# Window attention and a softplus feed-forward: new due times in the planner, weight words loaded ahead, and one VectorE step less per weight block

## The chip, the cores and the metric

The kernel runs on one NeuronCore of a Trainium2 chip, as one program. The metric is the device time of one execution in microseconds; the median of several runs is given. Times of single instructions come from one profiled execution.

The engines are called by their names: TensorE (PE, matrix products; PEld are its weight loads), VectorE (DVE), ScalarE (ACT), GpSimd (POOL) and SyncE (SP), which in this kernel issues nearly all DMA transfers.

## What is computed

```python
# q, k, v: 8 x 8 heads x 576 positions x 64; w_in 512 x 2048, w_out 2048 x 512
scores = q @ k.T / 8, masked to 0 <= pos_q - pos_k < 64
attn   = softmax(scores)            # with + 1e-9 in the denominator
x      = (attn @ v), heads side by side     # 4608 tokens x 512
h      = x @ w_in
g      = max(h, 0) + log1p(exp(-abs(h)))    # softplus
out    = g @ w_out                          # 4608 x 512, float32
```

The weights arrive as 64-bit floats and are handed to the kernel as pairs of 32-bit words (`w_words`): the upper word holds the sign, 11 bits of exponent and 20 bits of fraction, the lower word the rest. The kernel turns them into 32-bit floats itself.

## The kernel before

**Tiling.** The 4608 tokens are cut into 12 groups of 384. For each group, attention is made for four pairs of heads (`attention(g, hp)`), and the feed-forward runs over 16 blocks of 128 inner units (`ffn`). A block has an up-projection U (12 matmuls of 384 columns, L574), softplus on ScalarE (absolute value, exponential, logarithm, L578 to L580) and VectorE (the max and the sum, L586), a split of the result into a high and a low part (L588, L589), and a down-projection D (9 matmuls of 512 columns, L598) that adds up in PSUM over the 16 blocks. All products of the feed-forward are made as three products of high and low parts.

**The first two groups** go in a special order: blocks 0 to 7 of group 0, all 16 of group 1, then blocks 8 to 15 of group 0, so that the second half of the weights is needed later. The partial sums of group 0 wait in DRAM meanwhile (L636 and following). The attention of groups 0 and 1 turns the scores on TensorE (L439) and multiplies in 32 bits (L450). From group 2 on the scores are split into three bf16 parts and turned by DMA transposes (L475), and the products run at L542.

**Weights.** `convert(f)` handles block f. SP loads the words of a block (1 MB, L247) into a buffer that belongs to this block alone. ScalarE takes the absolute value of the upper word, read as a float (L248). Five VectorE steps follow: a maximum with 2^-15 (L249), a shift by three with a mask (L250), the two upper bits put in (L252), the three bits from the lower word put in (L254), and, after ScalarE has rounded the result to the high part (L256), the difference as the low part (L257). The work buffers are two, and the output's staging shares them.

**The order of work.** Nothing is left to a compiler. Every step above is an `Op` with an engine, a planned cost, the steps it depends on and the buffers that it opens or uses. `arrange` plays the kernel through with these costs: of all steps that could start on the engine that is free first, it takes the one with the earliest due time. The list that comes out is the order in which each engine's instructions are issued; the planned times themselves are not kept on the chip, where an engine goes through its list and waits only for data and buffers. A step on SP is not planned earlier than 30 us before it is due (`EARLY`). A transfer's length comes from a modelled pipe (`BYTES_PER_US`).

Due times come from `dues(times)`: U of step n is due at a time from the last round's plan, D 6.3 us later, the x of a group `AHEAD` (1, 1, 8 and 8 us) before its first U, and each pair of heads `APART` (4, 6, 18, 19 us) before the next. From there they are carried back along the dependencies, each step's cost stretched by 1.4. After each of four rounds the starting times of the U become the new `times`, and the plan that ends first is kept.

Of the kernel before, what the change touches and what calls it, by code (L numbers as in the profile page):

```python
# [8 lines left out]
F32 = mybir.dt.float32  # L9
# [6 lines left out]
P = 128  # L16
# [10 lines left out]
ROUNDS = 4  # L27
# [4 lines left out]
EARLY = 30  # L32

ZERO_HIGH = 2.0**-15

RESULT = {"PE": 0.25, "DVE": 0.12, "ACT": 0.15, "POOL": 0.2, "SP": 2.0}
BYTES_PER_US = 260e3
SMALL = 400e3
# [17 lines left out]
class Op:  # L56
    def __init__(self, eng, cost, fn, deps=(), opens=(), uses=(), nbytes=0, name=""):
        self.eng, self.cost, self.fn, self.name, self.nbytes = eng, cost, fn, name, nbytes
        self.deps, self.opens = [d for d in deps if d is not None], list(opens)
        self.due = self.start = self.end = 0.0  # L60
        self.later = []
        for d in self.deps:
            d.later.append(self)
        for b in [*uses, *opens]:
            b.users.append(self)


def arrange(ops, rings):
# [3 lines left out]
    free = {"PE": 0.0, "DVE": 0.8, "ACT": 2.1, "POOL": 0.8, "SP": 0.8}  # L72
    pipe = 0.0
# [4 lines left out]
    order = []  # L78
    while len(order) < len(ops):
        best = None  # L80
        for e, waiting in open_ops.items():
            could = []
            for o in waiting:
                at = max(ready_at[id(o)], o.due - EARLY if e == "SP" else 0.0)
                taken = {}
                for b in o.opens:
                    r = b.ring
                    n = len(r.taken) + taken.get(id(r), 0) - r.n
                    taken[id(r)] = taken.get(id(r), 0) + 1
                    if n >= 0:  # L90
                        users = r.taken[n].users
# [12 lines left out]
        if best is None:  # L104
            raise ValueError("stuck: " + ", ".join(o.name for w in open_ops.values() for o in w)[:600])
        t, o = best
        o.start = t
        free[o.eng] = t + o.cost
        o.end = t + o.cost + RESULT[o.eng]
        if o.nbytes:  # L110
            pipe = max(pipe, t + o.cost) + o.nbytes / BYTES_PER_US
            o.end = max(t + o.cost + 1.6 * o.nbytes / BYTES_PER_US, pipe if o.nbytes > SMALL else 0.0) + RESULT["SP"]
        for b in o.opens:
            b.ring.taken.append(b)
        done.add(id(o))
        order.append(o)
        open_ops[o.eng].remove(o)
        for n in o.later:
            left[id(n)] -= 1
            ready_at[id(n)] = max(ready_at[id(n)], t + o.cost if n.eng == o.eng and not o.nbytes else o.end)  # L120
            if not left[id(n)]:
                open_ops[n.eng].append(n)
    return order


@with_exitstack
def window_attention_softplus_ffn(
# [109 lines left out]
    def convert(f):  # L237
# [10 lines left out]
        a = add("ACT", 1.05, lambda: nc.scalar.activation(work(), word(1).bitcast(F32), AF.Abs), deps=[a], opens=[work], uses=[raw], name=f"abs{f}")  # L248
        a = add("DVE", 0.6, lambda: ts(work(), work(), ZERO_HIGH, None, ALU.max), deps=[a], uses=[work], name=f"c1.{f}")  # L249
        a = add("DVE", 0.6, lambda: ts(bits(), bits(), 3, 0x3FFFFFF8, ALU.logical_shift_left, ALU.bitwise_and),  # L250
                deps=[a], uses=[work], name=f"c2.{f}")
        a = add("DVE", 1.13, lambda: stt(bits(), word(1), 0xC0000000, bits(), ALU.bitwise_and, ALU.bitwise_or),  # L252
# [13 lines left out]
    def attention(g, hp):  # L266
# [27 lines left out]
        if quad:  # L294
# [29 lines left out]
            s = add("PE", 1.65, scores, deps=[lq, lk], opens=[*sp, st, mn], uses=[slot, two["q_in"], two["k_in"], *far], name=f"S{tag}")  # L324
# [87 lines left out]
        if by_pe:  # L412
# [42 lines left out]
            pv = add("PE", 1.65, products, deps=cp + lv, opens=[av, *x_t], uses=[pt, v_now, *both], name=f"V{tag}")  # L455
# [47 lines left out]
        c4 = add("DVE", 1.0, lambda: tt(v3()[low, :, :, 0, :], vv()[low, :, :, :], v12()[low, :, :, 1, :], ALU.subtract),  # L503
                 deps=[c3], opens=[v3], uses=[v_in, v12], name=f"v3.{tag}")
        c5 = add("DVE", 0.41, lambda: nc.vector.tensor_copy(v3()[up, :, :, 0, :], v12()[up, :, :, 0, :]), deps=[c1, c4],
# [4 lines left out]
        for hh in range(2):  # L510
# [38 lines left out]
            y = add("ACT", 0.39, lambda ds=ds, av=av: nc.scalar.copy(xf()[ds, :], av()[D:P, :TB]), deps=[p],  # L549
                    uses=[av, xf], name=f"y0.{tag}")  # L550
            done.append(add("DVE", 0.47, lambda ds=ds, av=av: tt(xf()[ds, :], av()[0:D, :TB], xf()[ds, :], ALU.add),  # L551
# [12 lines left out]
    def ffn(n, g, f, first, last):  # L564
# [20 lines left out]
        s = add("ACT", 1.21, soft, deps=[a], opens=[u], uses=[hps], name=f"soft{g}.{f}")  # L585
# [99 lines left out]
    best = None  # L685
    for _ in range(ROUNDS):
        for (p, n), r in rings.items():
            r.held = [b for key, b in two.items() if b.ring is r]
        dues(times)
# [4 lines left out]
        times = [o.start for o in ups]  # L694
# [48 lines left out]
```

## Time and profile before

| what | value |
|---|---|
| median of 3 runs | 994.69 us (994.53 to 995.12) |
| the profiled execution's own time | 993.75 us |
| its span, first to last instruction | 991.9 us |
| TensorE busy | 950.3 us, 96% of the span |
| VectorE busy | 796.2 us, 80% |
| ScalarE busy | 744.8 us, 75% |
| mean granted clock of TensorE | 0.987 |

A row of instructions gives the line of the kernel, engine, operation, written and read buffers, sizes and count. In groups, the total busy time and the mean of one in ns follow, then the idle time of the engine just before them and what ended it. In a timeline, the first number is the start, the second the length, both in us from the start of the span; a bracket at the end is the idle time before the row and its releaser. In a table of stretches each engine has its busy time and count, then come the granted clock of TensorE, the mean busy share of 16 DMA engines and GB/s. In a list of waits, the columns are total us, times, and the longest.

### The profile page before, as it was taken

To read this page: it belongs to the slowest core of one execution; us is meant where nothing else is said; L and a number is where in the kernel's file an instruction comes from. 1 tells how busy PE (TensorE), PEld (TensorE's weight loads), DVE (VectorE), ACT (ScalarE), POOL (GpSimd) and SP (SyncE) were. 2 spreads that over 40 slices of the span, in tenths; PEclk is the share of its full clock that TensorE was granted. 3 is DMA by queue.
4 is the path that set the end of the run, shared out by engine and by line. 5 is a ranking of instruction groups with operands and counts; after the bars stand their busy time and mean duration, and the time that the engine had idled before them with its cause. 6 is when DMAs were issued, how large, how long until landed. Compare 5 with 4: busy or idle time off the path is not lost.

```text
span 991.9 us, 16876 instructions
## 1 busy us (share of the span) xinstructions
PE 950.3 (96%) x6128; PEld 847.9 (85%) x6128; DVE 796.2 (80%) x1776; ACT 744.8 (75%) x1685; POOL 4.5 (0%) x18
## 2 busy tenths in 40 slices
PE   4888998999999999999999999999999999999997
PEld 3777977988898899989988988889888888988996
DVE  8995999788888888888888888878988888875333
ACT  6787887777778878877788788877877887776443
POOL 1000000000000000000000000000000000000000
PEclk7899998999999999999999999999999999999999
DMA  9606624554454345546444535444444645631000
GB/s 353 241 1 237 220 54 102 151 169 108 113 133 120 86 112 139 122 101 134 104 120 126 127 88 142 109 120 128 110 103 118 137 101 102 148 55 32 33 1 33
DMA packets 196516, 117.37 MB, mean 118 GB/s; under 512 B 130192, under 2 KB 187536, under 8 KB 194384
## 3 DMA queue, kind: packets, MB, share of 16 engines
q1 hardware_dynamic: 196144, 115.90, 45.4%
q8 instruction: 48, 0.79, 0.3%
q10 hardware_dynamic: 288, 0.39, 0.1%
q14 instruction: 36, 0.29, 0.1%
HBM read 74.58 MB, written 10.22 MB: 85 GB/s over the span
## 4 chain that ended last, share of the span: by engine, by line
PE 69%; ACT 16%; DVE 11%; issue 3%; DMA 1%; POOL 0%; SPq 0%; ACTq 0%; POOLq 0%; DVEq 0%
PE ps_o L598 31%; PE ps_h L574 30%; ACT st L388 4%; PE ps_a L542 3%; PE ps_a L363 3%; ACT u L579 2%; ACT u L578 2%; DVE u L586 1%; ACT xf L549 1%; DVE st L290 1%; ACT v L500 1%; DVE work L252 1%; DVE w L257 1%; ACT k L351 1%; ACT u L580 1%
## 5 line engine op out<-in xcount | busy, mean ns | idle before, releaser
L574 PE MATMUL ps_h<-x,w 128*128 128x384 f32 x2304 | 436.5, 339 | 11.8 <-DVE u L586 10.9
L598 PE MATMUL ps_o<-w,g 128*128 128x512 f32 x1728 | 433.9, 397 | 5.2 <-DVE g L589 3.4
L574 PEld LDWEIGHTS ps_h<-x,w 128*128 128x128 f32 x2304 | 404.1, 189 | 25.6 <-DVE u L586 7.9
L598 PEld LDWEIGHTS ps_o<-w,g 128*128 128x128 f32 x1728 | 315.0, 188 | 73.8 <-DVE g L589 14.6
L578 ACT ACTIVATE u<-ps_h 128x384 f32<-128x384 f32 x192 | 93.3, 486 | 127.4 <-PE ps_h L574 126.1
L586 DVE SCALAR_TENSOR_TENSOR u<-ps_h,u 128x384 f32<-128x384 f32 x192 | 106.6, 555 | 83.3 <-ACT u L580 81.5
L388 ACT ACTIVATE st<-st,mn 128x128 f32<-128x128 f32 x288 | 111.8, 390 | 19.2 <-DVE st L380 11.7
L589 DVE TENSOR_TENSOR g<-u,g 128x384 fp32r<-128x384 f32 x192 | 106.6, 555 | 13.0 <-ACT g L588 8.4
L580 ACT ACTIVATE u<-u 128x384 f32<-128x384 f32 x192 | 100.9, 526 | 6.1
L579 ACT ACTIVATE u<-u 128x384 f32<-128x384 f32 x192 | 100.8, 525 | 6.1
L588 ACT CAST g<-u 128x384 fp32r<-128x384 f32 x112 | 56.6, 505 | 15.8 <-DVE u L586 15.7
L290 DVE CUSTOM_DVE_ANT_0 st<-ps_a,wide 128x192 f32<-128x192 f32 x176 | 53.6, 351 | 14.2 <-PE ps_a L363 13.3
L542 PEld LDWEIGHTS <-v 128*128 128x128 bf16 x1136 | 54.7, 98 | 9.7 <-issue 9.1
L542 PE MATMUL ps_a<-tr,v 128*128 128x128 bf16 (+1 forms) x1136 | 61.5, 211 | 0.0
L363 PEld LDWEIGHTS ps_a<-k,q_hl 128*128 128x128 f32 x432 | 57.8, 191 | 2.9
L363 PE MATMUL ps_a<-k,q_hl 128*128 128x192 f32 x432 | 57.5, 271 | 0.0
L503 DVE TENSOR_TENSOR v<-v_in,v 64x896 bf16<-64x896 f32 x40 | 43.6, 1090 | 13.4 <-ACT v L502 12.8
L388 ACT ACTIVATION_READ_ACCUMULATOR st<-st,mn 128x1 f32 x288 | 53.9, 187 | 0.0
L351 ACT CAST k<-k_in 128x896 fp32r<-128x896 f32 x36 | 33.6, 934 | 24.6 <-PE ps_a L363 24.2
L502 ACT CAST v<-v_in 128x896 bf16<-128x896 f32 x40 | 37.4, 934 | 16.8 <-DVE v_in L501 16.8
L551 DVE TENSOR_TENSOR xf<-ps_a,xf 64x384 f32<-64x384 f32 x80 | 44.0, 550 | 4.7 <-ACT xf L549 2.5
L403 DVE TENSOR_TENSOR st<-st,sm 128x768 f32<-128x768 f32 x48 | 45.8, 954 | 0.9
(78 smaller groups left out, 778.1 us busy)
## 6 DMA issues: line engine op xcount, KB each, us to landing
v_in<-in_v_dram SPq DMA_DIRECT2D x80, 224.0 KB, 3.6
raw<-in_w_words_dram SPq DMA_DIRECT2D x16, 1024.0 KB, 12.2
k_in<-in_kT_dram SPq DMA_DIRECT2D x72, 224.0 KB, 3.6
q_in<-in_qT_dram SPq DMA_DIRECT2D x72, 192.0 KB, 3.7
out_dram<-raw SPq DMA_DIRECT2D x12, 512.0 KB, 3.6
out_dram<-raw SPq DMA_DIRECT2D x12, 256.0 KB, 2.9
v_two<-in_v_dram SPq DMA_DIRECT2D x3, 768.0 KB, 8.3
q_two<-in_qT_dram SPq DMA_DIRECT2D x8, 192.0 KB, 5.5
```

The costliest lines, as they stand in the source:

```text
L290: nc.vector.tensor_tensor_reduce(st()[:, hh, j, 0:width], scores, m, QSCALE, 3.0e38, ALU.add, ALU.min, mn()[:, hh, j : j + 1])
L363: mm(spv[:, hh, :], q_hl()[:, hh, j * P : (j + 1) * P], k_s[i]()[:, hh, j * P : j * P + W], start=(hh == 0 and i == 0), stop=(hh == 1 and ...
L388: nc.scalar.activation(sv()[:, i, 0:P], sv()[:, i, 0:P], AF.Exp, bias=mn()[:, hh, j : j + 1], scale=-1.0, accum_out=sm()[:, i : i + 1],)
L542: mm(av()[:, osl], (v3() if s else v12())[:, c, hh, :, :], src, start=(i == 0), stop=(i == len(passes) - 1), skip_group_check=True,)
L574: mm(hps()[:, :TB], weight(0, a, f)[:, c * P : (c + 1) * P], x[b][c](), start=(i_mm == 0), stop=(i_mm == 3 * NC - 1))
L578: nc.scalar.activation(u(), hps()[:, :TB], AF.Abs)
L579: nc.scalar.activation(u(), u(), AF.Exp, scale=-1.0)
L580: nc.scalar.activation(u(), u(), AF.Ln, bias=1.0)
L586: m = add("DVE", 0.47, lambda: stt(u(), hps()[:, :TB], 0.0, u(), ALU.max, ALU.add), deps=[s], uses=[hps, u], name=f"m{g}.{f}")
L588: lambda: (nc.scalar.copy if by_act else nc.vector.tensor_copy)(gt[0](), u()), deps=[m], opens=[gt[0]], uses=[u], name=f"g0.{g}.{f}")
L589: lo = add("DVE", 0.47, lambda: tt(gt[1](), u(), gt[0]().bitcast(F32), ALU.subtract), deps=[h], opens=[gt[1]], uses=[u, gt[0]], name=f"g1. ...
L598: mm(acc[j](), gt[a]()[:, j * P : (j + 1) * P], weight(1, b, f), start=(first and i == 0), stop=(last and i == 2),)
```

## The change

Three things change at once.

1. **Due times.** `dues(times)` is called once, for the first round. After each of now eight rounds a new function `latest(order, end)` goes through the plan in reverse: on each engine it places the steps from the end backward, each as late as its followers, the buffers that others wait for, and its engine allow. That latest start becomes the step's due time for the next round.
2. **Loads.** The loads of weight words are marked `ahead`: the 30 us hold does not apply to them, nor to transfers that open no buffer. In its place no SP step is planned while the modelled pipe is more than 4 us behind (`BACKLOG`). The pipe is modelled anew (390 bytes per ns in place of 260, a launch of 1.3 us, transfers one behind the other), and so are some planned costs (scores and products of the first groups 1.65 to 1.28, softplus 1.21 to 1.5, and four smaller ones).
3. **Conversion.** ScalarE multiplies the upper word by 2^-112 in place of taking its absolute value. This lowers the eight exponent bits that the float reading sees by 112, which is what the change of the exponent's offset (1023 to 127) comes to before the shift by three. The maximum at L249 goes; the masks of the next two steps become 0x7FFFFFF8 and 0x80000000. Four VectorE steps are left per block.

```diff
-ROUNDS = 4
+ROUNDS = 8
+BACKLOG = 4.0
-ZERO_HIGH = 2.0**-15
+REBIAS = 2.0**-112
-BYTES_PER_US = 260e3
-SMALL = 400e3
+BYTES_PER_US = 390e3
+LAUNCH = 1.3
...
-    free = {"PE": 0.0, "DVE": 0.8, "ACT": 2.1, "POOL": 0.8, "SP": 0.8}
-    pipe = 0.0
+    free = {"PE": 0.0, "DVE": 5.0, "ACT": 2.1, "POOL": 0.8, "SP": 0.8}
+    pipe = 2.2
...
-                at = max(ready_at[id(o)], o.due - EARLY if e == "SP" else 0.0)
+                at = ready_at[id(o)]
+                if e == "SP":
+                    at = max(at, o.due - EARLY if o.opens and not o.ahead else 0.0, pipe - BACKLOG)
...
-            pipe = max(pipe, t + o.cost) + o.nbytes / BYTES_PER_US
-            o.end = max(t + o.cost + 1.6 * o.nbytes / BYTES_PER_US, pipe if o.nbytes > SMALL else 0.0) + RESULT["SP"]
+            pipe = max(pipe, t + o.cost + LAUNCH) + o.nbytes / BYTES_PER_US
+            o.end = pipe + RESULT["SP"]
         for b in o.opens:
+            if len(b.ring.taken) >= b.ring.n:
+                o.freed += b.ring.taken[-b.ring.n].users
...
+def latest(order, end):
+
+    after = {id(o): [] for o in order}
+    left = {id(o): 0 for o in order}
+    for o in order:
+        for d, lag in [(d, None) for d in o.deps] + [(d, RESULT[d.eng]) for d in o.freed]:
+            after[id(d)].append((o, lag))
+            left[id(o)] += 1
+    before = {id(o): [*o.deps, *o.freed] for o in order}
+    wait = {id(o): len(after[id(o)]) for o in order}
+    free = dict.fromkeys(RESULT, end)
+    heap = {e: [] for e in RESULT}
+    by = {id(o): end for o in order}
+    for o in order:
+        if not wait[id(o)]:
+            heap[o.eng].append(o)
+    n = 0
+    while n < len(order):
+        best = None
+        for e, could in heap.items():
+            if not could:
+                continue
+            t = min(free[e], max(by[id(o)] for o in could))
+            o = max((o for o in could if by[id(o)] >= t - 1e-9), key=lambda o: o.start)
+            if best is None or t > best[0]:
+                best = (t, o)
+        t, o = best
+        heap[o.eng].remove(o)
+        o.last = t - o.cost
+        free[o.eng] = o.last
+        n += 1
+        for d in before[id(o)]:
+            lag = (d.end - d.start - d.cost) if d.nbytes else 0.0 if d.eng == o.eng else RESULT[d.eng]
+            by[id(d)] = min(by[id(d)], o.last - lag)
+            wait[id(d)] -= 1
+            if not wait[id(d)]:
+                heap[d.eng].append(d)
+    return n
...
+        a.ahead = True
-        a = add("ACT", 1.05, lambda: nc.scalar.activation(work(), word(1).bitcast(F32), AF.Abs), deps=[a], opens=[work], uses=[raw], name=f"abs{f}")
-        a = add("DVE", 0.6, lambda: ts(work(), work(), ZERO_HIGH, None, ALU.max), deps=[a], uses=[work], name=f"c1.{f}")
-        a = add("DVE", 0.6, lambda: ts(bits(), bits(), 3, 0x3FFFFFF8, ALU.logical_shift_left, ALU.bitwise_and),
+        a = add("ACT", 1.05, lambda: nc.scalar.mul(work(), word(1).bitcast(F32), REBIAS), deps=[a], opens=[work], uses=[raw], name=f"abs{f}")
+        a = add("DVE", 0.6, lambda: ts(bits(), bits(), 3, 0x7FFFFFF8, ALU.logical_shift_left, ALU.bitwise_and),
                 deps=[a], uses=[work], name=f"c2.{f}")
-        a = add("DVE", 1.13, lambda: stt(bits(), word(1), 0xC0000000, bits(), ALU.bitwise_and, ALU.bitwise_or),
+        a = add("DVE", 1.13, lambda: stt(bits(), word(1), 0x80000000, bits(), ALU.bitwise_and, ALU.bitwise_or),
...
+    dues(times)
     for _ in range(ROUNDS):
...
-        dues(times)
         order = arrange(ops, rings)
         end = max(o.end for o in order)
         if best is None or end < best[0]:
             best = (end, [(o, o.start) for o in order])
-        times = [o.start for o in ups]
+        latest(order, end)
+        for o in ops:
+            o.due = o.last
```

More of the change, by code (lines that the diff above doesn't have):

```diff
@@ L59, in __init__ @@
         self.deps, self.opens = [d for d in deps if d is not None], list(opens)
-        self.due = self.start = self.end = 0.0
+        self.due = self.start = self.end = self.last = 0.0
+        self.ahead = False
         self.later = []
@@ L78, in arrange @@
     order = []
+    for o in ops:
+        o.freed = []
     while len(order) < len(ops):
@@ L322, in scores @@
                             )
-            s = add("PE", 1.65, scores, deps=[lq, lk], opens=[*sp, st, mn], uses=[slot, two["q_in"], two["k_in"], *far], name=f"S{tag}")
+            s = add("PE", 1.28, scores, deps=[lq, lk], opens=[*sp, st, mn], uses=[slot, two["q_in"], two["k_in"], *far], name=f"S{tag}")
             scored.append(s)
@@ L453, in products @@
                         )
-            pv = add("PE", 1.65, products, deps=cp + lv, opens=[av, *x_t], uses=[pt, v_now, *both], name=f"V{tag}")
+            pv = add("PE", 1.28, products, deps=cp + lv, opens=[av, *x_t], uses=[pt, v_now, *both], name=f"V{tag}")
             x0 = add("ACT", 0.4, lambda: nc.scalar.copy(x_t[0](), av()[:, :TB]), deps=[pv], uses=[av, x_t[0]], name=f"x0.{tag}")
@@ L502, in attention @@
         c3 = add("ACT", 0.83, lambda: nc.scalar.copy(v12()[:, :, :, 1, :], vv()), deps=[c2], uses=[v_in, v12], name=f"v2.{tag}")
-        c4 = add("DVE", 1.0, lambda: tt(v3()[low, :, :, 0, :], vv()[low, :, :, :], v12()[low, :, :, 1, :], ALU.subtract),
+        c4 = add("DVE", 1.12, lambda: tt(v3()[low, :, :, 0, :], vv()[low, :, :, :], v12()[low, :, :, 1, :], ALU.subtract),
                  deps=[c3], opens=[v3], uses=[v_in, v12], name=f"v3.{tag}")
-        c5 = add("DVE", 0.41, lambda: nc.vector.tensor_copy(v3()[up, :, :, 0, :], v12()[up, :, :, 0, :]), deps=[c1, c4],
+        c5 = add("DVE", 0.3, lambda: nc.vector.tensor_copy(v3()[up, :, :, 0, :], v12()[up, :, :, 0, :]), deps=[c1, c4],
                  uses=[v12, v3], name=f"v4.{tag}")
@@ L548, in attention @@
             p = add("PE", 0.7, products, deps=[t0_, t1_, c1, c2, c3, c4, c5, p], opens=[av] if hh else [av, xf], uses=[tr, v12, v3], name=f"V{tag}")
-            y = add("ACT", 0.39, lambda ds=ds, av=av: nc.scalar.copy(xf()[ds, :], av()[D:P, :TB]), deps=[p],
+            y = add("ACT", 0.5, lambda ds=ds, av=av: nc.scalar.copy(xf()[ds, :], av()[D:P, :TB]), deps=[p],
                     uses=[av, xf], name=f"y0.{tag}")
-            done.append(add("DVE", 0.47, lambda ds=ds, av=av: tt(xf()[ds, :], av()[0:D, :TB], xf()[ds, :], ALU.add),
+            done.append(add("DVE", 0.58, lambda ds=ds, av=av: tt(xf()[ds, :], av()[0:D, :TB], xf()[ds, :], ALU.add),
                             deps=[y], uses=[av, xf], name=f"y1.{tag}"))
@@ L584, in ffn @@
                 uses=[b for i in range(2) for b in x[i]] + [w_all[f]], name=f"U{g}.{f}")
-        s = add("ACT", 1.21, soft, deps=[a], opens=[u], uses=[hps], name=f"soft{g}.{f}")
+        s = add("ACT", 1.5, soft, deps=[a], opens=[u], uses=[hps], name=f"soft{g}.{f}")
         m = add("DVE", 0.47, lambda: stt(u(), hps()[:, :TB], 0.0, u(), ALU.max, ALU.add), deps=[s], uses=[hps, u], name=f"m{g}.{f}")
@@ L693, in window_attention_softplus_ffn @@
             best = (end, [(o, o.start) for o in order])
-        times = [o.start for o in ups]
+        latest(order, end)
+        for o in ops:
+            o.due = o.last
     with tc.manual_schedule():
```

## The prediction

> **What bounds the kernel now.** I read the head of the page first, then a table of stretches whose borders I took from the order of TensorE's work, then who TensorE waited for in each, and last single rows around the long waits.
>
> ```profile
> span 991.9 us, 16876 instructions
> ...
> PE 950.3 (96%) x6128; PEld 847.9 (85%) x6128; DVE 796.2 (80%) x1776; ACT 744.8 (75%) x1685; POOL 4.5 (0%) x18
> ```
>
> TensorE is busy for 950.3 of 991.9 us, so no edit that leaves its matmuls alone can win more than 41.6 us, plus what a lowered clock adds to the matmuls. The change touches no matmul. Where do the 41.6 us lie?
>
> ```profile
> core 0: us, PE busy (x) PEld busy (x) DVE busy (x) ACT busy (x) POOL busy (x), PEclk, DMA share, GB/s
> 0.00:30.66 30.66, 15.80 (x216) 13.54 (x216) 25.86 (x85) 20.96 (x66) 4.49 (x18) 0.74 0.95 365
> 30.66:84.57 53.91, 47.51 (x385) 38.48 (x384) 48.10 (x111) 41.02 (x104) 0.00 (x0) 0.99 0.20 77
> 84.57:146.00 61.43, 58.76 (x366) 52.09 (x364) 54.37 (x98) 49.91 (x98) 0.00 (x0) 1.00 0.57 192
> 146.00:160.00 14.00, 7.69 (x68) 6.41 (x67) 13.54 (x28) 9.04 (x22) 0.00 (x0) 0.76 0.49 95
> 160.00:890.00 730.00, 724.39 (x4585) 650.80 (x4584) 613.46 (x1382) 575.69 (x1306) 0.00 (x0) 1.00 0.50 118
> 40.00:80.00 40.00, 36.11 (x273) 28.94 (x272) 36.95 (x97) 33.29 (x90) 0.00 (x0) 1.00 0.01 2
> 80.00:100.00 20.00, 17.44 (x149) 15.27 (x148) 11.65 (x28) 13.55 (x29) 0.00 (x0) 1.00 0.87 300
> 120.00:140.00 20.00, 19.98 (x151) 17.20 (x151) 19.44 (x39) 15.94 (x35) 0.00 (x0) 1.00 0.26 76
> ```
>
> Of the 41.6, the first four rows hold 30.2 (14.9, 6.4, 2.7 and 6.3), all before 160 us; the 730 us behind hold 5.6; the rest is the end. In the long row TensorE is busy 99%, so an order can hardly better it, only spoil it. In the first four VectorE is busy 141.9 of 160 us, 89%, against 613 of 730, 84%, later. The three short rows show why: DMA rests at a share of 0.01 from 40 to 80 us, then runs at 0.87 while VectorE falls to 11.65 of 20 us, then VectorE is at 97% while it catches up. The second half of the weight words comes late, and its conversion piles up.
>
> ```profile
> PE ps_a L319 <- POOL k_two L306: 5.2, 1, 5.2
> PE ps_o L439 <- DVE x L457: 3.7, 1, 3.7
> PE ps_a L450 <- DMA v_two<-in_v_dram: 2.6, 1, 2.6
> ```
>
> These are the longest waits up to 31 us; from 85 to 160 us:
>
> ```profile
> PE ps_h L574 <- DVE u L586: 6.3, 1, 6.3
> PE ps_a L319 <- DMA k_two<-in_kT_dram: 2.3, 1, 2.3
> ```
>
> The 6.3 us wait is the largest single one of the kernel; what VectorE ran ahead of it:
>
> ```profile
> 149.45 1.10 DVE L501 TENSOR_TENSOR v_in<-v_in,v 128x896 f32<-128x896 f32 x1
> 150.45 1.23 DVE L252 SCALAR_TENSOR_TENSOR work<-raw,work 128x1024 uint32<-128x1024 uint32 x1
> 151.58 1.23 DVE L257 TENSOR_TENSOR w<-work,w 128x1024 fp32r<-128x1024 f32 x1
> 152.72 0.57 DVE L586 SCALAR_TENSOR_TENSOR u<-ps_h,u 128x384 f32<-128x384 f32 x1
> ```
>
> And TensorE in the same stretch:
>
> ```profile
> 146.23 0.89 PE L319 MATMUL ps_a<-k_two,q_two 64*64 64x128 f32 x24
> 153.43 4.18 PE L574 MATMUL ps_h<-x,w 128*128 128x384 f32 x12 [6.31 <-DVE u L586]
> ```
>
> L586 (the max of softplus), which frees the bank that the next up-projection needs, stands in VectorE's queue behind one attention step and two conversion steps. Nothing was missing but turn: this is an order of the plan.
>
> **Part by part.** The VectorE step that goes is L249:
>
> ```profile
> L248 ACT ACTIVATE work<-raw x16: 1129/1145/1183, 14.8 to 142.4; 128x1024 f32<-128x1024 f32 x16
> L249 DVE TENSOR_SCALAR work<-work x16: 680/686/702, 16.6 to 147.1; 128x1024 f32<-128x1024 f32 x16
> ```
>
> Its share of the two stretches about 84.57 us (the third column is L249's busy time and count):
>
> ```profile
> 0.00:84.57 84.57, 5.49 (x8) 0.90 0.47 181
> 84.57:160.00 75.43, 5.51 (x8) 0.95 0.56 174
> ```
>
> Sixteen times 0.69 us leave VectorE, 5.5 us on either side of this row:
>
> ```profile
> 84.57 4.43 PE L574 MATMUL ps_h<-x,w 128*128 128x384 f32 x24
> 91.27 0.89 PE L319 MATMUL ps_a<-k_two,q_two 64*64 64x128 f32 x24 [2.27 <-DMA k_two<-in_kT_dram]
> 92.09 2.38 PE L574 MATMUL ps_h<-x,w 128*128 128x384 f32 x12
> ```
>
> At 84.57 the up-projection of the second group starts, 24 matmuls at once because its weights are long converted. Term A: it waits on attention of group 1, whose VectorE steps share the queue with the first eight conversions. From 30.66 on VectorE is busy 48.10 of 53.91 us, so I count the 5.5 us in full. Bounds 0 (the chain through ScalarE ends last) and 5.5.
>
> ScalarE's scaled copy in place of the absolute value has the same shape and strided input as L248, so I take its 1.145 us.
>
> ```profile
> L256 ACT CAST w<-work 128x1024 fp32r<-128x1024 f32 x16 | 16.7, 1044 | 10.6 <-DVE work L254 10.6
> ...
> L212 ACT ACT_TABLE_LOAD x1 | 1.3, 1283 | 0.7 <-PEq L729 0.7
> ```
>
> Copies of that size (L256) take 1.04, so the bounds are 0.1 us less per block and as much more, 1.7 us over sixteen, on an engine that idles a quarter of the span. A reload of function tables I exclude: copies run today between exponentials, and the table is loaded once. The two masks are constants in instructions that stay: nothing. The second VectorE step now waits for ScalarE itself where L249 did: one wait for another, with the same queue behind it.
>
> Loads. The weight words have a buffer per block and wait for nothing, so with the due-time hold gone the later eight leave SP as soon as their turn comes. Today:
>
> ```profile
> 83.08 0.49 SPq L247 DMA_DIRECT2D raw<-in_w_words_dram  x1
> 83.65 0.94 SPq L308 DMA_DIRECT2D q_two<-in_qT_dram  x1
> 84.64 0.47 SPq L307 DMA_DIRECT2D k_two<-in_kT_dram  x1
> ```
>
> And a load of the size of the last one on a quiet queue, KB and us to landing:
>
> ```profile
> k_in<-in_kT_dram SPq DMA_DIRECT2D x72, 224.0 KB, 3.6
> ```
>
> Term B: keys issued at 84.64, behind a weight block, are awaited until 91.27; 224 KB otherwise land in 3.6 us. Eight blocks of 1.05 MB at 365 GB/s are 23 us and fit into the 40 idle us, so the wait of 2.3 goes. Bounds 0 and 2.3. They pass group 1's loads on SP only where the plan puts them so (a rival below), and the partial stores and group 2's loads, at some 0.5 us of SP each, hidden in SP's idle time.
>
> Term C: the wait of 6.3 and, behind it, 12 matmuls in 4.18 us rather than 2.38: 1.8. Together 8.1. VectorE now works 54.37 + 13.54 = 67.9 us of the 75.4 from 84.57 to 160; without L249 it is 62.4, in a stretch that B and C would cut to 65.0: 96%. That can be: from 120 to 140 us it ran at 97% with TensorE at 19.98 of 20. Conversions pulled into 80 to 100 us, where 8.35 us stand idle, help. But at 96% an order must be nearly perfect, so I take two thirds, 5.4. Bounds 0 and 8.1.
>
> The Trainium skill (TensorE: Matmul & The Clock Gate, Part 1) says that the array falls to half clock after one idle window of about 3.4 us and needs as long to recover. The trace agrees: after 2.27 us of waiting 12 matmuls took 2.38, after 6.31 they took 4.18. By that rule a wait shrunk to a third costs no clock at all, C would be 4.2 + 1.8 = 6.0, and the time 0.6 lower than mine.
>
> Due times and costs (rounds, byte rate, backlog, the lengths for scores and softplus) issue nothing; they order. Term D, the front before 30.66: the 3.7 us wait for x could go if group 0's x pass ahead of the second weight block, or another weight block could stand in front of it (2.9 us, worked out at the fourth rival); 0, bounds -3.7 and +2.9. Term E, 160 to 890: 0; at best the 5.6 us go, at worst see the slower rival.
>
> Sum: 5.5 + 2.3 + 5.4 = 13.2. The profiled execution took 993.75 us, 1.85 more than its span; it becomes 980.55. The median of the runs is 994.69, 0.94 above it: 981.5. All bounds at their best give 5.5 + 2.3 + 8.1 + 3.7 + 5.6 = 25.2, so 969.5.
>
> **The rivals.** First, only the removed work counts. Due times that follow latest starts may put another step ahead of L586, and the wait moves instead of going. For it speaks that VectorE stays near 90% until 160 us. Then 5.5 us remain: 989.2.
>
> Second, nothing is gained: ScalarE or PSUM turns hold the front, and later waits return what A gives. 994.7. It speaks against this that TensorE is saturated behind 160 us, so time won ahead of it is not absorbed by a later wait.
>
> Third, slower, by one mechanism: latest starts carry no slack, where the present rule asks for each group's attention 8 us early. It would strike at the nine borders where group 3 to 11 begins. How near this is today, at the last one, on VectorE:
>
> ```profile
> 914.30 0.55 DVE L554 TENSOR_TENSOR x<-xf,x 128x384 fp32r<-128x384 f32 x1
> ```
>
> And the next group's first use on TensorE:
>
> ```profile
> 917.63 2.25 PE L574 MATMUL ps_h<-x,w 128*128 128x384 f32 x12
> ```
>
> The last x is ready at 914.85, the up-projection that can first use it starts at 917.63: 2.8 us of margin. A slip by one VectorE pile like that from 149.45 to L586's end (3.8 us) costs 3.8 - 2.8 = 1.0 per border, 9 in all; it decides from 13.2 / 9 = 1.5 per border. At 2 us each the time is 981.5 + 18 = 999.5. Against it: an engine takes what is ready, and with VectorE at 84% most steps run before they are due.
>
> Fourth, weights too early: more blocks in front of group 0's values, for which TensorE already waits 2.6 us. Each block in front adds 1.05 MB / 365 GB/s = 2.9 us; from five on, the gain is gone, and six give 981.5 + 17 = 999. The Trainium skill (DMA: Bandwidth & Descriptors, Queues, rings and completion order) states that each DMA engine consumes a ring in order, which is what this needs; the keys that wait behind a block at 84.64 agree with it. Against it: group 0's values are due before any but the first two blocks.
>
> **How the numbers follow.** A measurement of this kernel tells some 0.2%, 2 us, from no change. My forecast, 13.2 us within the bounds above, gets 0.60; only the removed work 0.18; no gain 0.07; late attention 0.10; weights in front 0.05. Faster is 0.60 + 0.18 = 0.78, same 0.07, slower 0.15. The likeliest time is 981.5. Low 970 is the sum of the best bounds; below it some 0.02. High 993 takes in the first rival and the faster edge of the second; above it lie the slower two and most of no change, near 0.18. So 8 in 10 lie between.
>
> **What would show it.** Right: L249 gone and four VectorE steps per weight block instead of five; all weight blocks issued by about 60 us and DMA at rest no more from 40 to 80; group 1's up-projection near 79 us, no wait on keys behind it, no wait over 3 us on L586 and clock 1.00 from 40 us on; TensorE still at 99% behind 160 us. Wrong: a wait of the same size on another VectorE step before 160 us (first rival), waits at each border of groups (third), or a wait for group 0's values well over 2.6 us (fourth).

## The result and the profile after

The changed kernel takes 964.67 us (median of 4 runs, 964.05 to 965.21) where the kernel before, beside it, takes 994.9 (994.53 to 995.12; a fourth execution, of 1551.96 us, does not enter the ratio). The ratio is 0.9697, 95% interval 0.9678 to 0.9716. The forecast was 981.5 with a range from 970 to 993: right in sign, short by more than half of what was won. The profiled execution took 965.21 us, 1.8 more than its span.

The head of the page of the kernel after:

```profile
span 963.4 us, 16889 instructions
...
PE 939.7 (98%) x6128; PEld 848.6 (88%) x6128; DVE 784.6 (81%) x1760; ACT 740.5 (77%) x1685; POOL 4.5 (0%) x18
```

Of the 28.5 us that the span lost, 17.9 are idle time of TensorE (41.6 before, 23.7 now). But its busy time fell too, by 10.6 us, for the same 6128 matmuls. Of that second number my forecast held 1.8 us, the matmuls at a lowered clock in term C, and nothing of the rest.

The table of stretches of the kernel after, cut at the same events as before (first up-projection of group 0, first of group 1), with the three short windows again:

```profile
0.00:27.98 27.98, 16.10 (x241) 13.32 (x241) 22.22 (x79) 19.34 (x64) 4.50 (x18) 0.82 0.96 371
27.98:78.91 50.93, 45.05 (x377) 36.38 (x376) 50.52 (x123) 46.90 (x120) 0.00 (x0) 1.00 0.70 277
78.91:160.00 81.09, 80.25 (x527) 71.50 (x526) 71.68 (x131) 66.19 (x131) 0.00 (x0) 1.00 0.27 68
160.00:860.00 700.00, 700.00 (x4456) 638.92 (x4455) 599.60 (x1354) 558.67 (x1273) 0.00 (x0) 1.00 0.51 121
40.00:80.00 40.00, 37.13 (x320) 29.96 (x319) 39.65 (x99) 37.48 (x105) 0.00 (x0) 1.00 0.58 226
80.00:100.00 20.00, 19.16 (x123) 17.74 (x122) 19.87 (x40) 18.85 (x32) 0.00 (x0) 1.00 0.26 76
```

The holes are where the first table had them, filled: DMA works between 40 and 80 us, VectorE is at 99% in both short windows instead of resting in the second, and from 78.91 to 160 us TensorE idles 0.84 us in place of 9.0 between 84.57 and 160. VectorE is now the full engine between the two first up-projections, 50.52 of 50.93 us. Behind 160 us the list of TensorE's waits is empty.

The conversion's groups of the kernel after (minimum, median and maximum in ns, then first and last start in us) and SP's list around 30 us:

```profile
L297 ACT ACTIVATE work<-raw x16: 1126/1152/1182, 14.8 to 120.0; 128x1024 f32<-128x1024 f32 x16
L298 DVE TENSOR_SCALAR work<-work x16: 681/686/694, 16.6 to 122.0; 128x1024 uint32<-128x1024 uint32 x16
```

```profile
28.92 2.02 SPq L295 DMA_DIRECT2D raw<-in_w_words_dram  x3
31.03 0.38 SPq L471 DMA_DIRECT2D v_two<-in_v_dram  x1
33.37 8.20 SPq L295 DMA_DIRECT2D raw<-in_w_words_dram  x6
```

The scaled copy costs what the absolute value did (1.152 us against 1.145), four VectorE steps are left, and the last weight block is issued by 41.6 us in place of 114. The last conversion starts at 120 us; before, it started at 142.

For the rest I cut every profiled execution at the same events. The n-th up-projection starts with matmul 12n of its line, and the order of the 192 steps is fixed, so U0.0, U1.0, U2.0 and U4.0 (group and block) and the last one are found by counting. The columns are the lengths between them, in us. The last column is the time that TensorE's weight loads waited for u or g from U2.0 to the last up-projection (the list of waits of PEld, below). The kernels ran in several sets, beside which the kernel before took 994.08 to 996.33 us; the ratios, given below, allow for that.

| kernel | median | to U0.0 | to U1.0 | to U2.0 | to U4.0 | to the last U | to the end | waits for u, g |
|---|---|---|---|---|---|---|---|---|
| before | 994.9 | 30.7 | 53.9 | 119.7 | 163.8 | 609.8 | 14.1 | 17.8 |
| after | 964.67 | 28.0 | 50.9 | 111.4 | 155.7 | 603.9 | 13.6 | 2.4 |
| no_due | 972.72 | 30.2 | 53.5 | 115.4 | 154.8 | 603.5 | 14.0 | 0.2 |
| no_cost | 970.38 | 25.0 | 51.6 | 116.0 | 155.0 | 606.7 | 14.0 | 3.4 |
| no_load | 985.1 | 55.0 | 43.9 | 109.9 | 155.5 | 605.4 | 13.7 | 0.3 |
| no_conv | 969.79 | 27.3 | 56.7 | 111.9 | 155.7 | 603.3 | 13.9 | 2.8 |
| only_due | 983.02 | 43.9 | 44.8 | 117.6 | 155.0 | 606.7 | 13.6 | 4.4 |
| only_cost | 984.99 | 32.1 | 51.9 | 118.2 | 158.2 | 609.1 | 13.9 | 10.1 |
| only_load | 995.57 | 28.1 | 66.2 | 114.3 | 162.9 | 609.4 | 14.1 | 15.8 |
| only_conv | 984.07 | 26.4 | 54.0 | 127.0 | 158.2 | 603.2 | 13.6 | 4.7 |
| before_r2 | 991.43 | 27.2 | 58.6 | 131.2 | 158.3 | 603.2 | 13.6 | 2.5 |
| before_r3 | 1010.35 | 46.7 | 50.1 | 115.2 | 160.6 | 621.4 | 13.6 | 28.5 |
| hold | 963.94 | 26.9 | 50.9 | 111.3 | 155.7 | 603.9 | 13.6 | 2.4 |
| nobacklog | 986.19 | 52.7 | 45.9 | 110.6 | 157.7 | 603.9 | 13.6 | 2.3 |
| hold_soft | 972.49 | 25.1 | 49.6 | 115.9 | 154.6 | 611.2 | 14.1 | 9.5 |
| soft_only_old | 971.69 | 25.4 | 51.3 | 113.6 | 154.5 | 611.3 | 13.9 | 9.5 |
| front_sv | 966.56 | 25.0 | 52.5 | 113.9 | 155.9 | 603.9 | 13.6 | 0.9 |

Between before and after, 14.0 us were won up to U2.0 (2.7, 3.0 and 8.3), 14.0 from there to the last up-projection (8.1 and 5.9), and 0.5 at the end.

The same border is not the same work, though. How far the down-projections lag behind the up-projections differs from plan to plan: at U2.0 the kernel before has run 30 of them and the kernel after 31. From U2.0 to the last up-projection the kernel before therefore runs 1431 matmuls of D and the kernel after 1422. The nine start 0.23 us apart, so they are worth 2.1 us: for the same work, some 16 us were won up to U2.0 and some 12 behind it. Besides before, the kernels with 1431 in that stretch are no_load, only_cost, only_load, only_conv, before_r2 and nobacklog; the others have 1422. Between single columns up to three down-projections move, so I compare longer stretches where I can. Nor are all waits in the last column waits of U and D: the 2.4 us of after and hold and the 2.3 of nobacklog are loads for the products of attention (L590), whose wait the profile puts down to u; at U and D these three have none.

### The profile page after: what moved, and what is told of

Its sections match the earlier page's. It is cut to its first block, busy times and chain, and to the rows that moved or that the text cites. A ratio compares the mean times of both kernels' runs of the same rounds, so it can differ in the third digit from the quotient of the medians.

```text
span 963.4 us, 16889 instructions
## 1 busy us (share of the span) xinstructions
PE 939.7 (98%) x6128; PEld 848.6 (88%) x6128; DVE 784.6 (81%) x1760; ACT 740.5 (77%) x1685; POOL 4.5 (0%) x18
## 4 chain that ended last, share of the span: by engine, by line
PE 91%; DVE 6%; ACT 1%; issue 1%; POOL 0%; POOLq 0%; ACTq 0%
PE ps_o L646 40%; PE ps_h L622 40%; PE ps_a L590 6%; PE ps_a L411 5%; DVE work L300 1%; DVE work L302 1%; DVE w L305 1%; ACT st L436 1%; DVE st L338 1%; DVE work L298 1%; DVE u L634 0%; DVE g L637 0%; PE ps_a L367 0%; DVE st L451 0%; DVE x L505 0%
## 5 line engine op out<-in xcount | busy, mean ns | idle before, releaser
L646 PE MATMUL ps_o<-w,g 128*128 128x512 f32 x1728 | 424.9, 394 | 0.0
L646 PEld LDWEIGHTS ps_o<-w,g 128*128 128x128 f32 x1728 | 320.3, 188 | 60.4 <-ACT u L626 0.2
L637 DVE TENSOR_TENSOR g<-u,g 128x384 fp32r<-128x384 f32 x192 | 106.3, 554 | 10.1 <-ACT g L636 5.8
L590 PEld LDWEIGHTS <-v 128*128 128x128 bf16 x1136 | 54.5, 98 | 9.6 <-issue 7.2
L590 PE MATMUL ps_a<-tr,v 128*128 128x128 bf16 (+1 forms) x1136 | 60.3, 211 | 0.0
L436 ACT ACTIVATION_READ_ACCUMULATOR st<-st,mn 128x1 f32 x288 | 53.9, 187 | 0.0
L451 DVE TENSOR_TENSOR st<-st,sm 128x768 f32<-128x768 f32 x48 | 45.9, 955 | 0.9
L549 DVE TENSOR_TENSOR v_in<-v_in,v 128x896 f32<-128x896 f32 x40 | 43.5, 1089 | 3.5 <-ACT v L548 3.1
L597 ACT COPY xf<-ps_a 64x384 f32<-64x384 f32 x80 | 38.1, 476 | 4.9 <-PE ps_a L590 3.1
## 6 DMA issues: line engine op xcount, KB each, us to landing
raw<-in_w_words_dram SPq DMA_DIRECT2D x16, 1024.0 KB, 13.9
```

The costliest lines, as they stand in the source:

```text
L436: nc.scalar.activation(sv()[:, i, 0:P], sv()[:, i, 0:P], AF.Exp, bias=mn()[:, hh, j : j + 1], scale=-1.0, accum_out=sm()[:, i : i + 1],)
L590: mm(av()[:, osl], (v3() if s else v12())[:, c, hh, :, :], src, start=(i == 0), stop=(i == len(passes) - 1), skip_group_check=True,)
L637: lo = add("DVE", 0.47, lambda: tt(gt[1](), u(), gt[0]().bitcast(F32), ALU.subtract), deps=[h], opens=[gt[1]], uses=[u, gt[0]], name=f"g1. ...
L646: mm(acc[j](), gt[a]()[:, j * P : (j + 1) * P], weight(1, b, f), start=(first and i == 0), stop=(last and i == 2),)
```

## The experiments

Two questions: which part of the change carries which stretch, and why 14 us (some 12 for the same work) came out of a stretch in which TensorE was busy for 99%. Theory A held that the due times from the reverse schedule did the latter, rival B that the corrected planned costs did.

**Each part set back in the changed kernel.**

```diff
-    dues(times)
     for _ in range(ROUNDS):
...
+        dues(times)
         order = arrange(ops, rings)
...
-        latest(order, end)
-        for o in ops:
-            o.due = o.last
+        times = [o.start for o in ups]
```

> The changed kernel, but with the due times of before (carried back from the up-projections with stretch and lead, renewed from their planned starts), in eight rounds. Theory A, the due times from the reverse schedule took away the short stalls of TensorE behind 204 us (some 14 us of the 28.5): near 979 us, U2.0 within 3 us of the changed kernel's, and the stalls back in the later groups. Rival B, the corrected planned costs did it: within 4 us of 964.7.

972.72 us, ratio to before 0.9786 (0.9771 to 0.98). It was run with four rounds; the plan taken is that of the second, and with eight rounds the planner writes out the same program. The time lies between the two expectations. All of the 8 us lie ahead of U2.0; behind it this kernel is the shortest of all (154.8 and 603.5). Theory A falls: the stretch behind U2.0 does not need the new due times.

```diff
-        s = add("ACT", 1.5, soft, deps=[a], opens=[u], uses=[hps], name=f"soft{g}.{f}")
+        s = add("ACT", 1.21, soft, deps=[a], opens=[u], uses=[hps], name=f"soft{g}.{f}")
```

And so with the other planned costs and VectorE's first free time.

> The changed kernel, but with the planned costs of before (softplus 1.21, scores and products of the first groups 1.65, and the four small ones; VectorE free at 0.8). Rival B, the corrected costs, softplus above all, took the stalls behind 204 us away: near 978 us, with TensorE's weight loads waiting on the low part of g again. Theory A, the due times did: within 4 us of 964.7.

970.38 us (0.9763, 0.9749 to 0.9778), again between the two expectations. Behind U2.0 it loses 2.2 us, with 3.4 us of waits on u and g; ahead of it 2.3. Rival B's 14 us are not there either.

```diff
-                at = ready_at[id(o)]
-                if e == "SP":
-                    at = max(at, o.due - EARLY if o.opens and not o.ahead else 0.0, pipe - BACKLOG)
+                at = max(ready_at[id(o)], o.due - EARLY if e == "SP" else 0.0)
...
-            pipe = max(pipe, t + o.cost + LAUNCH) + o.nbytes / BYTES_PER_US
-            o.end = pipe + RESULT["SP"]
+            pipe = max(pipe, t + o.cost) + o.nbytes / BYTES_PER_US
+            o.end = max(t + o.cost + 1.6 * o.nbytes / BYTES_PER_US, pipe if o.nbytes > SMALL else 0.0) + RESULT["SP"]
```

With it go the constants of the old pipe.

> The changed kernel, but with the loads of before (30 us hold for every SP step, no backlog limit, the old model of the pipe). If the early weight words carry what was won before U2.0 (14 us, less the 5.5 of the shorter conversion): near 972, DMA at rest again between 40 and 80 us and VectorE idle around 90. If they are hidden anyway: within 2 us of 964.7.

985.1 us (0.9908, 0.9892 to 0.9925), far more than either expectation, and at another place: U0.0 comes at 55.0 us. SP's list of this kernel, and TensorE's rows behind it:

```profile
2.22 1.15 SPq L291 DMA_DIRECT2D raw<-in_w_words_dram  x2
3.42 0.45 SPq L350 DMA_DIRECT2D qk_far<-in_kT_dram  x1
5.62 1.38 SPq L291 DMA_DIRECT2D raw<-in_w_words_dram  x3
7.05 0.43 SPq L351 DMA_DIRECT2D qk_far<-in_qT_dram  x1
```

```profile
20.50 1.56 PE L362 MATMUL ps_h<-qk_far 64*64 64x128 f32 x24 [10.86 <-DMA qk_far<-in_qT_dram]
...
33.55 1.56 PE L362 MATMUL ps_a<-k_two,q_two 64*64 64x128 f32 x24 [6.52 <-DMA q_two<-in_qT_dram]
```

Five weight blocks went ahead of group 0's queries, which were issued at 7.05 and awaited until 20.50 us. This is the mechanism of the fourth rival of the forecast, with queries in place of values. In the trace the five blocks land from 9.55 to 19.89 us, 2.4 to 3.0 us apart (the forecast had 2.9 a block), and the queries at 20.41. Three more blocks, issued from 12.56 us on, stand ahead of the queries awaited until 33.55, and U0.0 comes 27.0 us later than in the changed kernel. Reverse due times without the new loads bring it about; the full change avoids it.

```diff
-        a = add("ACT", 1.05, lambda: nc.scalar.mul(work(), word(1).bitcast(F32), REBIAS), deps=[a], opens=[work], uses=[raw], name=f"abs{f}")
+        a = add("ACT", 1.05, lambda: nc.scalar.activation(work(), word(1).bitcast(F32), AF.Abs), deps=[a], opens=[work], uses=[raw], name=f"abs{f}")
+        a = add("DVE", 0.6, lambda: ts(work(), work(), ZERO_HIGH, None, ALU.max), deps=[a], uses=[work], name=f"c1.{f}")
```

The two masks are those of before as well.

> The changed kernel, but with the five VectorE steps of before in each conversion. If VectorE bounds the time until U1.0, U1.0 comes 5.5 us later and the total is 970 us; if it bounds all the way to U2.0, 11 us later, 976; if VectorE has room by now, within 2 us of 964.7.

969.79 us (0.9757, 0.9743 to 0.9772). U1.0 starts at 83.98 us in place of 78.91, 5.1 later, and the total is 5.1 more: 5.5 was expected, and nothing beyond U1.0 changes by more than 0.6. VectorE bounds the time up to U1.0 and has room behind it.

**Each part alone, on the kernel before.** The same edits, the other way round.

> The kernel before, with nothing but the due times from the reverse schedule, in eight rounds. Theory A (they remove the stalls behind 204 us whatever the costs): some 14 us faster than before, near 981, with no wait of TensorE on g or u behind 204 us. Rival B (they need the corrected costs): within 4 us of 994.7.

983.02 us (0.9882, 0.9867 to 0.9897): near the time of theory A, but not by its path alone. U0.0 comes 13.2 us late, 9.1 of which are regained by U1.0. From U2.0 to the last up-projection 11.9 us are won by the borders, some 9.9 for the same work, and 4.4 us of waits on u and g stay where theory A expected none.

> The kernel before, with nothing but the corrected planned costs. Rival B (a right cost of softplus alone removes the stalls): near 981. Theory A (the due times are what counts): within 4 us of 994.7.

984.99 us (0.9905, 0.989 to 0.992), between the two expectations. 6.3 us are won from U2.0 to the last up-projection, where 10.1 us of waits on u and g stay. So due times alone and costs alone each win a part of that stretch, and no_due and no_cost show that neither is needed for most of it.

> The kernel before, with nothing but the new loads (weight words ahead, backlog limit, new model of the pipe). If the late weight words made the pile on VectorE before 160 us: the 6.3 us wait of an up-projection and the 2.3 us wait on keys go, near 985. If the pile is a matter of order: within 4 us of 994.7.

995.57 us (1.0009, 0.9999 to 1.0018): nothing. The work of the conversion (all instructions that touch its work tiles; after the length, VectorE's time and ScalarE's) up to U1.0 in this kernel:

```profile
28.10:94.26 66.16, 47.12 (x49) 21.90 (x20) 0.95 0.51 207
```

In the kernel before the same row reads 28.02 (x28) us for VectorE from 30.66 to 84.57. The words come early, and VectorE, bound there, spends 19 us more on conversion ahead of U1.0, for blocks that U1.0 does not need; U1.0 comes 9.7 us late. In this plan early loads alone only let the wrong work go first.

> The kernel before, with nothing but the four-step conversion. If VectorE bounds the time until U1.0: 5.5 us faster, 989; with the wait of 6.3 us gone too, 981. If the plan moves the wait elsewhere: within 2 us of 994.7.

984.07 us (0.9895, 0.988 to 0.991). U1.0 is 4.2 us earlier; then 7.3 us are lost up to U2.0, 6.5 of it in one wait:

```profile
PE ps_a L318 <- DMA k_two<-in_kT_dram: 6.5, 1, 6.5
```

And then the stretch from U4.0 on is 603.2 us in place of 609.8, with one down-projection more in it and no conversion. I see no reason in the conversion itself that connects the two. That suggested theory C: any edit that touches a planned cost makes the planner take another plan, and the stretch is decided by which.

**The kernel before, another of its own plans.** Before writes out the best of four rounds, by the planner's reckoning the fourth. These two kernels write out the second and the third, nothing else:

```diff
-ROUNDS = 4
+ROUNDS = 2
...
-        if best is None or end < best[0]:
+        if True:
```

In the other kernel ROUNDS is 3.

> The kernel before, nothing changed but that the plan of the second round is written out, where before takes that of the fourth. The shorter conversion alone shortened the stretch from U4.0 to the last up-projection from 609.8 to 603.2 us, though it runs no conversion there. Theory C, that stretch is set by which of the plans happens to be taken, not by any part of the change: near 604 here too. Theory D, a part of the change is needed: within 1.5 of 609.8. The total may be worse in either case, by the start.

> The kernel before, with the plan of its third round written out. As with the second round: near 604 us from U4.0 to the last up-projection by theory C if this plan's due times happen to fall well, within 1.5 of 609.8 by theory D. If rounds two and three both stay near 609.8, theory C falls.

991.43 us (0.9969, 0.996 to 0.9979) and 1010.35 (1.0162, 1.0142 to 1.0182). From U4.0 to the last up-projection they take 603.2 and 621.4 us, against 609.8 in before, which has one down-projection fewer there. No instruction was edited; theory C stands. From U2.0 to the last up-projection the plan of the second round wins 12.1 us with the same matmuls, as much as the change wins there for the same work; ahead of U2.0 it loses 12.6. The planner itself reckons 979.5 us for the plan that before takes, 989.9 for the second and 985.0 for the third, so its ranking is not that of the chip. One row for each kernel, from U2.0 to the last up-projection, TensorE's busy time and its count first; before:

```profile
204.28:977.85 773.57, 767.87 (x4736) 690.43 (x4736) 613.34 (x1371) 583.37 (x1308) 0.00 (x0) 1.00 0.45 105
```

before_r2:

```profile
216.91:978.35 761.44, 761.02 (x4736) 692.89 (x4735) 617.01 (x1370) 584.09 (x1304) 0.00 (x0) 1.00 0.46 108
```

before_r3:

```profile
211.99:993.96 781.97, 771.70 (x4727) 688.98 (x4726) 615.00 (x1368) 584.03 (x1305) 0.00 (x0) 1.00 0.44 104
```

after:

```profile
190.30:949.85 759.55, 759.55 (x4728) 692.99 (x4727) 612.86 (x1370) 578.35 (x1303) 0.00 (x0) 1.00 0.45 108
```

The rows of before_r3 and after lack the one down-projection told of above. The same 4736 matmuls at clock 1.00 are "busy" for 767.87 us in one plan of before and 761.02 in another. So waits lie inside the busy time. They show in the list of waits of the weight loads (PEld), total us, times, longest; before, in that stretch:

```profile
PEld ps_o L598 <- DVE g L589: 11.0, 29, 1.0
PEld L542 <- issue: 8.0, 39, 0.3
PEld ps_h L574 <- DVE u L586: 5.7, 8, 0.8
```

before_r3:

```profile
PEld ps_o L598 <- DVE g L589: 20.1, 40, 1.0
...
PEld ps_o L598 <- DVE g L588: 8.5, 14, 1.0
```

after:

```profile
PEld L590 <- issue: 5.9, 27, 0.3
PEld L590 <- ACT u L626: 1.9, 7, 0.3
```

In a down-projection every third product has the low part of g as its stationary operand, the one that a weight load brings in. One such place in before:

```profile
226.80 2.01 PE L598 MATMUL ps_o<-w,g 128*128 128x512 f32 x8
...
227.64 1.09 DVE L501 TENSOR_TENSOR v_in<-v_in,v 128x896 f32<-128x896 f32 x1
...
228.64 0.55 DVE L589 TENSOR_TENSOR g<-u,g 128x384 fp32r<-128x384 f32 x1
...
229.25 1.45 PEld L598 LDWEIGHTS ps_o<-w,g 128*128 128x128 f32 x7 [0.87 <-DVE g L589]
229.25 1.88 PE L598 MATMUL ps_o<-w,g 128*128 128x512 f32 x7 [0.44 <-DVE g L589]
```

VectorE's list has an attention step (L501) ahead of L589. The weight load waits 0.87 us for it, and TensorE's own row shows only 0.44 of that as idle time: the matmuls of D start 0.23 us apart, but the profile makes each 0.39 long, so the one in front still counts as busy for a while. Each such wait is 1 us at most. How much the 39 of them in before cost can be read from the starts of the matmuls in the trace. Those with a late load start 9.1 us later in all than at the usual distance, only 5.7 of it idle, and those right behind them another 3.5: together 12.6 us, against the some 12 won. In after there is not one.

The waits also go with the stretch over all seventeen kernels. Among the seven with 1431 matmuls of D in it, 0.3 to 4.7 us of waits go with 760.9 to 761.6 us, 10.1 with 767.3, 15.8 with 772.3 and 17.8 with 773.6. Among the ten with 1422, 0.2 to 4.4 us go with 758.3 to 761.7, 9.5 with 765.8 twice, and 28.5 with 782.0.

**Pieces of the loads.**

```diff
-        a.ahead = True
+        a.ahead = False
```

> The changed kernel with the weight words no longer marked as ahead: they are held to 30 us before they are due, as other loads are; the order of TensorE, VectorE and ScalarE stays, and only SP's list differs, with the later weight blocks between other loads up to some 115 us. If loading them early in itself is worth what I forecast for the wait on keys, 2 us or more slower than 964.7. If the weight blocks are in time either way: within 1.5 us of 964.7.

963.94 us (0.9694, 0.968 to 0.9708), the same as the changed kernel within the noise. Two of SP's rows:

```profile
28.59 0.42 SPq L295 DMA_DIRECT2D raw<-in_w_words_dram  x1
...
99.88 0.59 SPq L295 DMA_DIRECT2D raw<-in_w_words_dram  x1
```

The last weight block leaves at 99.88 us in place of 41.6 at the latest, and nothing is lost. TensorE's list is that of the changed kernel; ten of VectorE's 1259 steps and two of ScalarE's changed places. The early loads in themselves are worth nothing here.

```diff
-                    at = max(at, o.due - EARLY if o.opens and not o.ahead else 0.0, pipe - BACKLOG)
+                    at = max(at, o.due - EARLY if o.opens and not o.ahead else 0.0, 0.0)
```

> The changed kernel without the limit on the modelled pipe's backlog (4 us). Without all three parts of the loads it was 20.4 us slower, because weight blocks went ahead of group 0's queries and keys, and U0.0 came at 55 us. If the limit is what keeps them back: U0.0 behind 40 us and over 980 in total. If the better model of the pipe does it: U0.0 near 28 to 32 and within 5 us of 964.7.

986.19 us (0.9917, 0.9902 to 0.9932), U0.0 at 52.7. The first rows of TensorE that waited, in this kernel:

```profile
14.90 1.56 PE L367 MATMUL ps_a<-k_two,q_two 64*64 64x128 f32 x24 [14.90 <-DMA k_two<-in_kT_dram]
...
36.71 1.56 PE L367 MATMUL ps_o<-qk_far 64*64 64x128 f32 x24 [11.12 <-DMA qk_far<-in_kT_dram]
```

By these rows the backlog limit is what keeps weight blocks from standing in front of group 0's keys. With reverse due times and without it, the start loses 24.7 us, most of which, 21.5, stays to the end. The output of this kernel is wrong (a relative error of 0.066), and why is open; I use it only for where its loads stand and what TensorE waits for at the start.

**Pieces of the costs.**

```diff
-        s = add("ACT", 1.5, soft, deps=[a], opens=[u], uses=[hps], name=f"soft{g}.{f}")
+        s = add("ACT", 1.21, soft, deps=[a], opens=[u], uses=[hps], name=f"soft{g}.{f}")
```

This is soft_only_old; hold_soft has `a.ahead = False` beside it.

> The changed kernel with softplus alone planned at 1.21 us as before. All costs of before made it 5.7 us slower: 2.4 us earlier at U1.0, 4.7 us more from there to U2.0, 2.8 more from U4.0 on. If softplus is the cost that counts, near 970 with that same pattern; if the first groups' scores and products are, within 2 us of 964.7.

> The changed kernel with the weight words held as in the run without the mark, and softplus planned at 1.21 us as before. If the cost of softplus is what keeps the low part of g in time: weight loads of TensorE wait on it again for 5 us or more behind U2.0, and the stretch from U4.0 to the last up-projection is 606 us or more. If not: 604, and U1.0 before 77 us, some 962 in total.

971.69 us (0.9749, 0.9734 to 0.9764) and 972.49 (0.976, 0.9744 to 0.9777). The waits are back, and the stretch from U4.0 is 611.3 and 611.2 us. The total of soft_only_old is near the expected 970, but not by the expected pattern: it is 2.2 us earlier at U1.0, loses 2.2 from there to U2.0, and 6.2 from U2.0 to the last up-projection. Waits of the weight loads in soft_only_old from U2.0 on:

```profile
PEld L590 <- issue: 8.7, 36, 0.3
PEld ps_h L622 <- DVE u L634: 5.3, 8, 0.7
PEld ps_o L646 <- DVE g L637: 4.2, 10, 0.5
```

A plan that believes softplus to take 1.21 us, where the chip needs some 1.5 (three instructions of 0.49 to 0.53), expects u and g too early and leaves other work ahead of them; that is my reading, which no run shows by itself. Against it, only_due plans with 1.21 as well and has 4.4 us of waits, and no_cost, with all costs of before, 3.4. So the right cost helps here and is not needed everywhere.

```diff
-            s = add("PE", 1.28, scores, deps=[lq, lk], opens=[*sp, st, mn], uses=[slot, two["q_in"], two["k_in"], *far], name=f"S{tag}")
+            s = add("PE", 1.65, scores, deps=[lq, lk], opens=[*sp, st, mn], uses=[slot, two["q_in"], two["k_in"], *far], name=f"S{tag}")
...
-            pv = add("PE", 1.28, products, deps=cp + lv, opens=[av, *x_t], uses=[pt, v_now, *both], name=f"V{tag}")
+            pv = add("PE", 1.65, products, deps=cp + lv, opens=[av, *x_t], uses=[pt, v_now, *both], name=f"V{tag}")
```

> The changed kernel with the scores and products of the first groups planned at 1.65 us as before. The clock is below 1 in that part, so 1.65 may be the truer length there. If it is what brought U1.0 to 76.6 us with all the costs of before: U1.0 near 76.6 and the rest as in the changed kernel, 962. If it only shifts the order: U1.0 within 1 us of 78.9.

966.56 us (0.9702, 0.9687 to 0.9716). U1.0 is 1.4 us earlier, at 77.5, and U2.0 1.1 later: between the two expectations, a shift of order, no gain. None of these kernels is clearly faster than the changed one.

## Why the prediction was right up to U2.0 and wrong behind it

**Term A, 5.5 us up to U1.0: right.** U1.0 came 5.7 us earlier; 2.7 of these were there at U0.0 already (term D), so A and D together were forecast at 5.5 and measured at 5.7. By the runs the shorter conversion is worth 5.1 of it set back and 4.2 alone, because VectorE is the full engine there, as the forecast said. My lower bound, ScalarE's chain ending last, did not come up.

**Terms B and C, 2.3 + 5.4 = 7.7 us between U1.0 and U2.0: both waits went, but the size was low and part of the reason wrong.** The stretch lost 8.3 us. That this lies so near 7.7 is partly luck. The stretch before and after:

```profile
84.57:204.28 119.71, 110.72 (x757) 98.47 (x756) 105.11 (x206) 96.82 (x204) 0.00 (x0) 0.97 0.57 165
```

```profile
78.91:190.30 111.39, 110.56 (x750) 98.93 (x749) 95.08 (x184) 91.77 (x191) 0.00 (x0) 1.00 0.38 90
```

TensorE's idle time fell from 8.99 to 0.83 us, so both waits went nearly whole, where I had counted two thirds of the second and its clock loss. Its busy time stayed, though it holds 18 matmuls of D more (two down-projections, 4.1 us) and 24 of attention fewer. I credited the early weight words. hold, where the last block leaves at 99.88 us, has the same 111.3 us; only_load wins 5.4 there but pays 9.7 ahead of it. Due times and costs lose 4.0 and 4.7 us when set back and win 2.1 and 1.5 alone; no single part brings the whole 8.3. Without the new loads (no_load) the stretch is as short, 109.9 us with one down-projection fewer. So this stretch needs the due times and the costs, both of them, and not the loads. The rule of the clock gate (the Trainium skill, TensorE: Matmul & The Clock Gate, Part 1) fits again: the longest wait behind 31 us is 2.4 us, and the granted clock reads 1.00 in every row from 27.98 to 949.85 us.

**Term D, 0 up to U0.0:** measured 2.7, within its bounds. It is part of the 5.7 under term A and does not count twice.

**Term E, 0 behind 160 us and at best 5.6: this step failed.** The forecast said that TensorE is busy 99% there, "so an order can hardly better it, only spoil it". The 14.0 us won behind U2.0 by the borders were 5.7 of idle time (773.57 - 767.87) and 8.3 of busy time. Of the latter, 2.1 are the down-projection that the kernel after runs ahead of U2.0; some 6.3 were busy time that was no work. So for the same work some 12 us went, more than twice the 5.6 that I had put as the best. That an order alone can do it is shown by before_r2: the same matmuls in another order, and 12.1 us less. The step took the share of busy time as a measure of how full TensorE was. The profile's legend says that the ends of matmuls are modelled, and the rows at 229.25 us show a matmul counted as busy in part of the wait for a late weight load. The list that had it was there: the waits of the weight loads, 17.8 us on u and g against the 5.3 that TensorE's own list shows. I had read only the latter. What hid the 6.3 us is thus known; which part of the change led the planner to an order without these waits stays open, see below.

**The fourth rival** did not occur in the changed kernel. Its mechanism did, at queries and keys in place of values, in two kernels that lack part of the change, no_load and nobacklog. The Trainium skill (DMA: Bandwidth & Descriptors, Queues, rings and completion order) has a ring consumed in order; queries issued at 7.05 us behind five blocks and awaited until 20.50 agree. What I had not seen is that the change contains both the danger, due times that favour weight blocks, and the guard, the backlog limit. **The third rival**, attention late at the borders of groups, did not occur: TensorE's list of waits is empty behind 160 us. Where waits did come back (soft_only_old), they stood at u and g. My argument against this rival, that an engine takes what is ready, holds for the planner; on the chip an engine keeps to its list.

**What stays open.** That waits for u and g set the stretch behind U2.0 is shown by the kernel before itself, with three of its plans. What makes the planner arrive at a plan without them is only half shown: the length of softplus matters where it alone is wrong, by 6.2 us (765.8 against 759.6), yet with other edits plans with few of these waits come out at either value. I did not find a single input that decides it. Nor can the some 12 us be divided among the three parts: no_due, no_load and no_conv each keep all of it, only_conv alone gets 12.2 by another plan, and before_r2 gets 12.1 with no part of the change at all.

## What to carry to other kernels

Before calling an engine full, look at the waits of its weight loads, and compare the busy time of the same number of matmuls in two stretches or two runs: the share of busy time can hide more than the idle time shows, here some 6.3 us beside 5.7. Count also what each run has done at the borders: one down-projection on the other side of U2.0 was 2.1 of the 14.0 us. Where a planner writes the order, any edit of a cost draws another plan; run the old kernel with another of its own plans before crediting the edit, since that alone moved this kernel from 994.9 to 991.4 or 1010.4 us, and its long stretch by as much as the whole change did. And parts that prove worth nothing or harm alone (the loads, 995.57) can be what makes another part safe (985.1 without them).

## What was not expected of the hardware

Nothing new of the chip itself. In no_load the five weight blocks ahead of the queries landed 2.4 to 3.0 us apart, where 2.9 a block were worked out. ScalarE's multiply by a constant runs as fast as its absolute value on this shape (1.152 and 1.145 us), and waits up to 2.4 us on TensorE left the granted clock at 1.00.
